# A long-convolution and MLP kernel: the second stage's table spread on chip in both halves, the second filter half turned by DMA transposes, the first inverse of half 0 on 64-row TensorE tiles

## The chip, the cores and the metric

The kernel runs on one core of one Trainium2 chip. The metric is the device time of one execution in microseconds (us). Before the change three runs gave 236.3, 236.95 and 237.21 us, a median of 236.95 us. The profile is of one execution.

## What is computed

Sequence length S = 2048, width D = 512, hidden width F = 1376, all arrays bfloat16. Two blocks A and B are applied twice, with the same weights both times:

```python
def _A_ref(q, k, v, shift_k, ssm_k, ssm_D):
    ...
    for t in range(ks):                      # ks = 4 taps
        k_shift = k_shift + k_pad[:, t:t + S, :] * shift_k[:, ks - 1 - t][None, None, :]
    kv = k_shift * v
    ...                                      # kv and ssm_k padded to 2 S, real FFTs
    y_f = kv_f * kf_f[None, :, :, :]
    y = irfft2(y_f)[..., :S, :]              # a long convolution along S, per channel
    y = y + kv * ssm_D[None, None, :]
    return q * y

def _B_ref(x, w1, b1, w2, b2):
    y = _layernorm(x, axis=-1)
    h = _gelu(einsum("bsd,df->bsf", y, w1) + b1)
    return einsum("bsf,fd->bsd", h, w2) + b2

x = A_q
x = x + _A_ref(_layernorm(x), A_k, A_v, A_shift_k, A_ssm_k, A_ssm_D)
x = x + _B_ref(_layernorm(x), B_w1, B_b1, B_w2, B_b2)
x = x + _A_ref(_layernorm(x), A_k, A_v, ...)
x = x + _B_ref(_layernorm(x), ...)
```

The convolution's result y depends on k, v and the filter only, so it is computed once and used by both A blocks.

## The kernel before

**Halves.** The sequence is split into two halves of 1024 positions. Half 0 needs the transform of filter half 0 and of data half 0; half 1 needs those and the transforms of filter half 1 and data half 1. Once y of half 0 is there, the LayerNorms and the MLP of half 0 run, in blocks of 128 or 256 rows, while the convolution of half 1 is computed beside them; then the MLP of half 1 runs in blocks of 512 rows.

**Stages, by the tags in the code.** `ht0`, `ht1`: the filter half is loaded with channels on the partitions and turned, 8 TensorE transposes to a tile (`turn`, L561), four tiles to a half, each copied out of PSUM by ScalarE or VectorE. `fir0` to `fir3`: the key of half 0 is turned (L610), shifted and mixed by its taps (L635) and multiplied by v (L641, VectorE). `h1_0`, `x1_0`, `h1_1`, `x1_1`: first transform stage (`stage1`, L578), eight tiles of 16 matmuls each. `h2_0`, `x2_0`, `h2_1`, `x2_1`: second stage (`stage2`, L590), eight tiles of 16 matmuls, whose weights are a table of 16384 columns in `R_S2`. A second stage's tiles 0 to 3 read its first 8192 columns and tiles 4 to 7 the others. Then come the products (L475, 128x1024 in half 0), the first inverse stage (`inverse1`, L695, tags `i1_0` and `i1_1`, eight tiles) and the second (`inverse2`, L717). ScalarE (L480) or VectorE (L481) copies each tile out of PSUM; such a copy is called an eviction here. The products also need the filter's spectrum with its real and imaginary parts exchanged, which eight DMAs make from SBUF to SBUF (`swap`, L460 `ar<-ar`).

**The table.** Every eighth block of 16 columns of `R_S2` belongs to the partitions p with p mod 8 = d, and is zero elsewhere. The compact form `C2` has 2048 columns. Before, the first half of the table is made on chip: the first 1024 columns of `C2` are loaded to `R_C` and eight instructions (tag `spread`, L519 on ScalarE, L520 on VectorE) multiply them by a mask, one for each d. The second half, 8192 columns, comes from HBM in eight loads of 256 KB (`tab_s`).

**`inverse1`** has two forms. In the whole form a tile is 16 matmuls of 128 rows by 128 columns; in the split form it is 32 matmuls on two halves of 64 rows, which write less:

```python
if split:
    for g in range(2):
        ins.append((512 * g + 4 * i, n, A(64 * g, 64, o, [4, 128]), A(64 * g, 64, R_U + n * 128 + 4 * g, [8, 16], [1, 4])))
else:
    ins.append((i * 128, n, A(0, 128, o, [4, 128]), A(0, 128, R_U + n * 128, [1, 128])))
```

Before, half 0 uses the whole form and half 1 the split one.

**What sets the order.** `Prog` records every operation. `SEQ` lists their numbers in the order in which each engine's queue is filled; `ENGS` says, one letter each, which engine takes an operation that several can do; `BANKS` gives each PSUM tile its bank. `sync` then derives the semaphore waits. Each engine works through its queue strictly in order. All large DMAs are issued by SyncE (SP), also in order, so a DMA that waits holds back those behind it. On GpSimd (POOL) each instruction waits for the one ahead of it.

**The MLP.** `m1` (L920) is the first matrix product, evicted with the GELU by ScalarE (L925); `m2` (L954) the second, added to x by VectorE (L958). The rows are normalised by L856 (ScalarE) or L857 (VectorE), after statistics by L831 and L832 (VectorE) and three small POOL instructions (L836, L838, L846). `q`, `y`, `z` are the tags of the first LayerNorm, of the multiplication with y, and of the second LayerNorm; the first two row blocks, `z0` and `z1`, are turned on TensorE (L908), all later ones by DMA transposes (L900).

Of the kernel before, what the change touches and what calls it, by code (L numbers as in the profile page):

```python
# [36 lines left out]
class Prog:  # L37
# [312 lines left out]
def _tables():  # L350
# [5 lines left out]
    a = np.arange(8)  # L356
# [12 lines left out]
    for j in range(8):  # L369
        m = np.arange(128) % 8 == pd[j]  # L370
        S2[m, :, j] = C2.reshape(128, 128, 16)[m]
    S2 = np.concatenate([C2, S2.reshape(128, 16384)], 1)
    ph = TWO_PI * k2[:, None] * a[None, :] / 8
    c, s = np.cos(ph), np.sin(ph)
    U = np.zeros((2, 8, 8, 2, 8, 2, 8))
# [23 lines left out]
def bass_interleave_layers__ssm_conv_h3__mixer_channel_mlp__prompt_kernel(  # L399
        nc, A_q, A_k, A_v, A_shift_k, A_ssm_k, A_ssm_D, B_x, B_w1, B_b1, B_w2, B_b2, out):  # L400
    P = Prog(nc)
# [593 lines left out]
```

## Time and profile before

| what | value |
|---|---|
| median of the timed runs | 236.95 us (236.3 to 237.21) |
| span of the profiled execution | 234.0 us; no other time is listed for that execution, so what lies around the span is taken as 236.95 - 234.0 = 2.95 us |
| TensorE (PE) busy | 222.7 us, 95% |
| VectorE (DVE) busy | 178.7 us, 76% |
| ScalarE (ACT) busy | 164.5 us, 70% |
| GpSimd (POOL) busy | 55.5 us, 24% |
| DMA | 24.93 MB in 40106 packets |
| granted TensorE clock | 1.00 throughout |

The span runs from the first to the last instruction. A busy share is an average over stages: in the first 60 us three engines take turns to be the last, and only the stage's own rows tell which. In a row of the timeline the numbers are the start, the time until the last of the merged instructions ended, the engine, the line, the operation, output and input, and the count; behind it stands the idle time ahead of it, with what ended it.

### The profile page before, as it was taken

Reading aid. Unit: us, or ns where it says so; the run is one execution under the profiler, and the core shown is the slowest. Engines: PE = TensorE matmul, PEld = TensorE weight load, DVE = VectorE, ACT = ScalarE, POOL = GpSimd, SP = SyncE. Lnnn points to the kernel's source line nnn. Section 1 sums busy time; section 2 is a strip of 40 time slices with the busy share of each in tenths; the row PEclk is TensorE's granted clock in tenths of the full one; section 3 lists DMA queues with packets and bytes.
Section 4 is the critical chain, followed back from the end, with each engine's and each line's share of the span. In section 5 each row is a group of like instructions: output and inputs, shape, how many; then the busy total and the mean of one; then the engine's idle time right before and its main releaser. Section 6 shows DMA issues by size and latency. Waiting matters only on the chain.

```text
span 234.0 us, 6498 instructions
## 1 busy us (share of the span) xinstructions
PE 222.7 (95%) x2743; PEld 147.1 (63%) x2765; DVE 178.7 (76%) x362; ACT 164.5 (70%) x262; POOL 55.5 (24%) x113
## 2 busy tenths in 40 slices
PE   7989887999999999999999999999999999999995
PEld 3878776967868596677966576644444444444454
DVE  0699998999999999999999988781777569410222
ACT  2789999989968688999879986488058216802710
POOL 2270132006403405639303331204011120200000
PEclk9999999999999999999999999999999999999999
DMA  6999489928994360033500313401300130170202
GB/s 185 381 386 305 147 229 274 324 65 150 144 211 126 70 158 3 1 48 72 155 4 3 90 24 68 134 3 22 69 0 3 28 62 0 23 115 0 90 0 92
DMA packets 40106, 24.93 MB, mean 107 GB/s; under 512 B 23591, under 2 KB 33677, under 8 KB 40077
## 3 DMA queue, kind: packets, MB, share of 16 engines
q1 hardware_dynamic: 39778, 24.36, 39.7%
q8 instruction: 22, 0.36, 0.7%
q10 hardware_dynamic: 298, 0.16, 0.4%
q14 instruction: 8, 0.06, 0.1%
HBM read 13.23 MB, written 2.10 MB: 66 GB/s over the span
## 4 chain that ended last, share of the span: by engine, by line
PE 58%; DVE 24%; ACT 10%; issue 2%; POOL 2%; DMA 2%; SPq 0%; DVEq 0%
PE ps L920 23%; PE ps L954 23%; DVE ar L475 13%; ACT ar L480 9%; PE ps L695 4%; DVE sm L831 3%; PE ps L590 2%; DMA ar<-in_A_ssm_k_dram 2%; DVE ar L672 2%; DVE ar L958 2%; DVE ar L641 2%; PE ps L717 1%; POOL sm L836 1%; PE ps L578 1%; PE ps L635 1%
## 5 line engine op out<-in xcount | busy, mean ns | idle before, releaser
L925 ACT ACTIVATE ar<-ps,sm 128x256 bf16<-128x256 f32 (+5 forms) x143 | 65.7, 523 | 33.2 <-PE ps L920 32.9
L920 PE MATMUL ps<-ar 128*128 128x256 bf16 (+5 forms) x569 | 81.9, 297 | 0.4 <-ACT ar L480 0.2
L480 ACT ACTIVATE ar<-ps 128x1024 bf16<-128x1024 f32 (+3 forms) x77 | 71.1, 998 | 11.0 <-PE ps L578 3.4
L954 PE MATMUL ps<-ar 128*128 128x512 bf16 (+1 forms) x323 | 75.9, 379 | 1.5 <-issue 0.6
L920 PEld LDWEIGHTS ps<-ar 128*128 128x128 bf16 (+1 forms) x572 | 52.9, 100 | 27.5 <-ACT ar L480 1.1
L475 DVE TENSOR_TENSOR ar<-ar 128x512 bf16<-128x512 bf16 (+2 forms) x104 | 62.7, 646 | 1.5 <-ACT ar L480 0.8
L954 PEld LDWEIGHTS ps<-ar 128*128 128x128 bf16 (+1 forms) x341 | 32.4, 98 | 35.3 <-ACT ar L925 0.4
L958 DVE TENSOR_TENSOR ar<-ar,ps 128x512 bf16<-128x512 bf16 x31 | 20.8, 680 | 32.9 <-PE ps L954 32.9
L831 DVE BATCH_NORM_STATS2 sm<-ar 128x6 f32<-128x512 bf16 x64 | 42.5, 685 | 0.5
L856 ACT ACTIVATE ar<-ar,sm 128x512 bf16<-128x512 bf16 x39 | 30.6, 813 | 12.9 <-DVE sm L843 8.8
L836 POOL TENSOR_SCALAR sm<-sm 128x2 f32<-128x2 f32 (+2 forms) x22 | 9.9, 449 | 89.0 <-DVE sm L832 88.8
L838 POOL TENSOR_TENSOR sm<-sm 128x2 f32<-128x2 f32 (+2 forms) x26 | 21.7, 834 | 25.1 <-DVE sm L836 23.1
L590 PE MATMUL ps<-ar 128*128 128x64 bf16 x512 | 18.4, 193 | 1.5 <-DVE ar L481 0.7
L578 PE MATMUL ps<-ar 128*64 128x128 bf16 x512 | 17.9, 221 | 1.8 <-ACT ar L480 1.2
L590 PEld LDWEIGHTS ps<-ar 128*128 128x128 bf16 x512 | 16.8, 98 | 3.6 <-DVE ar L481 1.3
L578 PEld LDWEIGHTS ps<-ar 128*64 128x64 bf16 x512 | 14.9, 110 | 4.8 <-ACT ar L480 1.9
L481 DVE CAST ar<-ps 128x1024 bf16<-128x1024 f32 x12 | 14.6, 1218 | 1.2 <-PE ps L578 0.9
L846 POOL TENSOR_SCALAR sm<-sm 128x1 f32<-128x1 f32 x34 | 15.1, 460 | 1.6
L695 PE MATMUL ps<-ar 64*128 64x64 bf16 (+1 forms) x384 | 12.4, 203 | 1.0 <-DVE ar L475 0.9
L695 PEld LDWEIGHTS ps<-ar 64*128 64x128 bf16 (+1 forms) x384 | 11.8, 113 | 2.2 <-DVE ar L475 1.0
L857 DVE TENSOR_SCALAR ar<-ar,sm 128x512 bf16<-128x512 bf16 x25 | 10.3, 415 | 2.7 <-POOL sm L846 2.5
L788 DVE SCALAR_TENSOR_TENSOR ar<-ar,sm,ps 128x512 bf16<-128x512 bf16 x16 | 11.1, 740 | 0.3 <-PE ps L590 0.3
(45 smaller groups left out, 93.5 us busy)
## 6 DMA issues: line engine op xcount, KB each, us to landing
ar<-ar SPq DMA_DIRECT2D x16, 256.0 KB, 4.0
ar<-tab_s SPq DMA_DIRECT2D x9, 256.0 KB, 6.3
ar<-in_A_ssm_k_dram SPq DMA_DIRECT2D x8, 256.0 KB, 5.9
ar<-in_A_q_dram SPq DMA_DIRECT2D x8, 256.0 KB, 4.4
ar<-in_A_v_dram SPq DMA_DIRECT2D x8, 256.0 KB, 5.0
out_dram<-ar SPq DMA_DIRECT2D x7, 256.0 KB, 2.5
ar<-in_B_w_dram SPq DMA_DIRECT2D x4, 344.0 KB, 5.2
ar<-in_B_w_dram SPq DMA_DIRECT2D x5, 256.0 KB, 5.2
```

The source lines that it names most:

```text
L475: return P.op(eng, lambda e: e.tensor_tensor(o, a, b, op), dur, reads=[a, b] + list(more), writes=[o])
L480: return e.activation(dst, src(), AF.Copy)
L578: r = e.matmul(Q(tl, 64 * ri, 64, i * 128, [1, 128]), w, m, start=True, stop=True)
L590: r = e.matmul(Q(tl, 0, 128, i // 8 * 512 + i % 8 * 4, [32, 16], [1, 4]), w, m, start=True, stop=True)
L695: r = e.matmul(Q(tl, 0, 128, i, *([32, 16], [1, 4]) if split else ([1, 128],)), w, m, start=n == 0, stop=n == 1)
L831: P.op(DVE, lambda e, sj=sj, x=x: e.bn_stats(sj, x), 600.0, reads=[x], writes=[sj])
L838: P.op(POOL, lambda e: e.tensor_tensor(r, v, hf, ALU.pow), 420.0 + 149.0 * n, reads=[v, hf], writes=[r])
L856: return e.activation(o, x, AF.Identity, bias=u, scale=r)
L920: r = e.matmul(Q(tl, 0, rows, 0, [1, w]), a, m, start=dk == 0, stop=dk == 3)
L925: P.op(ACT, lambda e, dst=dst, tl=tl, rows=rows, bias=bias, w=w: e.activation(dst, Q(tl, 0, rows, 0, [1, w]), AF.Gelu_apprx_tanh, bias=bia ...
L954: r = e.matmul(Q(tl, 0, 128, 0, [1, 512]), ins[fc][0], ins[fc][1], start=fc == 0, stop=fc == 10)
L958: P.op(DVE, lambda e, x=x, tl=tl: e.tensor_tensor(x, x, Q(tl, 0, 128, 0, [1, 512]), ALU.add), 604.0, reads=[x], writes=[x], tile=tl)
```

## The change

1. **Table.** Both halves of `R_S2` are spread on chip. The eight loads of the second half go; one load of the other 1024 compact columns comes. There are 16 `spread` instructions in place of 8, and POOL is now among the engines that can run them.
2. **Filter half 1.** `turn(1, ...)`, with its four TensorE tiles of 8 transposes and their four evictions, is replaced: the load puts the rows in another order, four POOL copies (tag `hcopy`, 128x1024, read with a stride of 8 elements) gather them into `R_Y0`, and eight DMA transposes, two to a copy, turn them into `R_HP1`. `h1_1` reads its weights from there with a stride.
3. **First inverse of half 0** uses the split form.
4. `SEQ`, `ENGS` and `BANKS` are new throughout. Lines move by 6 to 13 in the file (L590 is L596 after, L695 is L701, L475 is L476).

```diff
     SEQ = (
-        0, 46, 8, 45, 35, 2, 6, 3, 5, 36, 12, 9, 1, 10, 11, 25, 4, 44, 217, 7, 56, 197, 15, 50, 16, 57, 14, 13, 47,
...
+        44, 36, 46, 37, 45, 9, 0, 18, 1, 38, 47, 57, 39, 43, 40, 41, 3, 6, 2, 48, 58, 59, 7, 51, 4, 74, 22, 202, 221,
...
-    S2 = np.concatenate([C2, S2.reshape(128, 16384)], 1)
+    S2 = C2
...
     def load_h(half, o):
         for b in range(4):
-            dma(A(0, 128, o + b * 1024, [1, 1024]), dr(A_ssm_k, b * 128 * 2048 + 1024 * half, [2048, 128], [1, 1024]), 1 << 18, paced=True)
+            rows = [[2048, 128]] if not half else [[2048, 8], [8 * 2048, 16]]
+            dma(A(0, 128, o + b * 1024, [1, 1024]), dr(A_ssm_k, b * 128 * 2048 + 1024 * half, *rows, [1, 1024]), 1 << 18, paced=True)
...
-    tload(t_s2, 18432, 0, R_C, 1024)
+    wide = 2048
+    for h in range(2):
+        tload(t_s2, wide, 1024 * h, R_C + 1024 * h, 1024)
...
-    for i in range(8, 16):
-        tload(t_s2, 18432, 2048 + i * 1024, R_S2 + i * 1024, 1024)
...
-    for h in range(1):
+    for h in range(2):
         for d in range(8):
...
-            P.op(BOTH, f, {ACT: 912.0, DVE: 395.0}, reads=[c, m], writes=[o])
+            P.op((ACT, DVE, POOL), f, {ACT: 1040.0, DVE: 395.0, POOL: 1050.0}, reads=[c, m], writes=[o])
...
-    turn(1, R_HRAW1, R_HP1)
+    P.tag = "hcopy"
+    for b in range(4):
+        o, x = A(0, 128, R_Y0 + 1024 * b, [128, 8], [1, 128]), A(0, 128, R_HRAW1 + 1024 * b, [1, 8], [8, 128])
+        P.op(POOL, lambda e, o=o, x=x: e.tensor_copy(o, x), 1050.0, reads=[x], writes=[o])
+    P.tag = "ht1"
+    for b in range(4):
+        for i in range(2):
+            x, o = A(0, 128, R_Y0 + 1024 * b + 512 * i, [1, 512]), A(0, 128, R_HP1 + 1024 * b + 512 * i, [128, 4], [1, 128])
+            P.op(SP, lambda e, x=x, o=o: e.dma_start_transpose(o, x), 1300.0, reads=[x], writes=[o], dma=True, nbytes=1 << 17)
+    lhs = lambda g: A(0, 128, R_HP1 + 1024 * (g // 16) + g % 16, [16, 64])
     P.tag = "h1_1"
-    stage1(lambda g: A(0, 128, R_HP1 + 64 * g, [1, 64]), R_G1)
+    stage1(lhs, R_G1)
...
-    inverse1(R_1, R_2, R_3, False)
+    inverse1(R_1, R_2, R_3, 1)
```

The key's eight DMA transposes of half 1 move into a function `turn_k`, called once at the same place.

Three places show what the new order does. **POOL, ahead of the second stage.** Before, behind the last of the bias additions to the filter (L475, 1x16x8) and of the tap products (L548), POOL has only small work:

```order
L475 TENSOR_TENSOR ar<-ar 1x16x8
L548 TENSOR_TENSOR ar<-ar 128x256
L624 COPY ar<-ar 128x3
L836 TENSOR_SCALAR sm<-sm 128x1
L838 TENSOR_TENSOR sm<-sm 128x1
L624 COPY ar<-ar 128x3
L838 TENSOR_TENSOR sm<-sm 128x1
```

After the change the same stretch of POOL's queue holds spreads (L526, 128x64x16) and gathering copies (L753, 128x1024):

```order
L526 TENSOR_SCALAR ar<-ar,sm 128x64x16 x2
L849 TENSOR_SCALAR sm<-sm 128x1
L851 TENSOR_TENSOR sm<-sm 128x1
L859 TENSOR_SCALAR sm<-sm 128x1
L788 CAST sm<-ar 128x1
L526 TENSOR_SCALAR ar<-ar,sm 128x64x16
L630 COPY ar<-ar 128x3
L476 TENSOR_TENSOR ar<-ar 1x16x8
L526 TENSOR_SCALAR ar<-ar,sm 128x64x16 x3
L753 COPY ar<-ar 128x1024
L526 TENSOR_SCALAR ar<-ar,sm 128x64x16 x5
L849 TENSOR_SCALAR sm<-sm 128x2
```

Eleven of the 16 spreads now stand on POOL, four on DVE and one on ACT (before, six on DVE and two on ACT). The first three and the first of the run of three complete POOL's part of the table's first half; the other seven, with one gathering copy among them, complete its part of the second.

**SP, around the eight exchanges** (`ar<-ar 64x8x256`). Before, they go out in two groups of four, with loads between and behind them:

```order
L460 DMA ar<-in_A_ssm_k_dram 128x1024
L460 DMA ar<-in_B_b_dram 96x1
L460 DMA ar<-ar 64x8x256 x4
L460 DMA ar<-in_B_w_dram 128x2x512
L460 DMA ar<-ar 64x8x256 x4
L470 DMA ar<-tab_small 128x1024
```

After the change the DMA transposes of the filter (L758) stand among them:

```order
L758 DMA_TRANSPOSE ar<-ar 128x4x128
L461 DMA ar<-in_B_b_dram 96x1
L461 DMA ar<-ar 64x8x256 x4
L758 DMA_TRANSPOSE ar<-ar 128x4x128 x2
L461 DMA ar<-ar 64x8x256 x3
L758 DMA_TRANSPOSE ar<-ar 128x4x128 x2
L461 DMA ar<-ar 64x8x256
L461 DMA ar<-in_B_w_dram 128x1376
```

Two transposes are now ahead of the second group, and four ahead of the last exchange.

**PE, from the second stage to the second inverse.** Before (L590 second stage, L578 first stage of filter half 1, L561 its transposes, L695 first inverse, L717 second inverse):

```order
L590 MATMUL ps<-ar 128x16x4 x48
L578 MATMUL ps<-ar 64x128 x64
L561 MATMUL ps<-ar 128x128 x8
L695 MATMUL ps<-ar 128x128 x128
L578 MATMUL ps<-ar 64x128 x32
L717 MATMUL ps<-ar 128x512 x2
L578 MATMUL ps<-ar 64x128 x16
L717 MATMUL ps<-ar 128x512 x14
```

After (L596, L584, L701 and L723 are the same stages):

```order
L596 MATMUL ps<-ar 128x16x4 x16
L584 MATMUL ps<-ar 64x128 x48
L701 MATMUL ps<-ar 128x16x4 x64
L584 MATMUL ps<-ar 64x128 x16
L701 MATMUL ps<-ar 128x16x4 x192
L584 MATMUL ps<-ar 64x128 x32
L723 MATMUL ps<-ar 128x512 x4
L584 MATMUL ps<-ar 64x128 x16
L723 MATMUL ps<-ar 128x512 x12
```

The last of the three first-stage tiles directly ahead of the first inverse needs the third pair of filter transposes. Behind the second inverse both programs run the same tiles, except that the turning of `z1` (L908, L921 after) now stands ahead of the first `m1` tile and stood behind it. `z0` and `z1` are normalised by ACT after the change; before, `z0` was normalised by DVE.

More of the change, by code (lines that the diff above doesn't have):

```diff
@@ L44 @@
     SEQ = (
[55 rows of a table removed]
[56 rows of a table added]
     ENGS = (
[L101 to L103 removed]
+            "vpvvappvpppppppvpvpvpvpvpaaavaavavvaaavaaavaappppaaavaaavvvaaaaaaaaavaaaavaaaavaaaaaaappppaaaaaaaaaaaaaa"
+            "aaaaaaaaaaaaaaappappaavpvppaappvvppaappaappaappaapvaappaappaapvaappaappaappavppvvppvavpavavvvvavvvvavvav"
+            "pvvvappvavavvaavapvvavapvvvvv")
     BANKS = (
[L105 to L107 removed]
+            "42272442460200460002067635640040262422640464246244600602604062234024424622264600444260620624204042204043"
+            "30461456547705110517010666612614320037722232405172756007426335436147461307413422270727065155362103103451"
+            "4060364405475615411270347042152307163024542756001300612716327433526516701532367")
     def __init__(self, nc):
@@ L502, in load_t, with turn_k @@
             dma(A(0, 128, o + 512 * a, [1, 512 * w]), dr(x, 512 * (1024 * half + a), [8 * 512, 128], [1, 512 * w]), w << 17, paced=True)
-    tload(t_s2, 18432, 0, R_C, 1024)
+    wide = 2048
+    for h in range(2):
+        tload(t_s2, wide, 1024 * h, R_C + 1024 * h, 1024)
     load_h(0, R_1)
+    def turn_k(half):
+        for a in range(8):
+            src, dst = dr(A_k, 512 * (1024 * half + a), [8 * 512, 128], [1, 512]), A(0, 128, R_KT + 144 * a + 16, [1152, 4], [1, 128])
+            P.op(SP, lambda e, src=src, dst=dst: e.dma_start_transpose(dst, src), 1300.0, writes=[dst], dma=True, nbytes=1 << 17)
     load_t(A_k, 0, R_8, 2)
     load_t(A_v, 0, R_8 + 4096, 2)
-    for i in range(8, 16):
-        tload(t_s2, 18432, 2048 + i * 1024, R_S2 + i * 1024, 1024)
     P.tag = "spread"
@@ L797, in bass_interleave_layers__ssm_conv_h3__mixer_channel_mlp__prompt_kernel @@
     P.tag = "kt"
-    for a in range(8):
-        src, dst = dr(A_k, 512 * (1024 + a), [8 * 512, 128], [1, 512]), A(0, 128, R_KT + 144 * a + 16, [1152, 4], [1, 128])
-        P.op(SP, lambda e, src=src, dst=dst: e.dma_start_transpose(dst, src), 1300.0, writes=[dst], dma=True, nbytes=1 << 17)
+    turn_k(1)
     for c in (0, 2):
```

6 lines of the change are left out of this document (removed), and 109 rows, old and new, of the table SEQ.

## The prediction

> **What bounds the kernel now.** I read the busy shares by stage first, then each engine's timeline around the point where the MLP begins, then single rows for prices. The first view gives the busy time of PE, PEld, DVE, ACT and POOL in six stretches (length, then busy us and count), the clock and the DMA share.
>
> ```profile
> 8.00:20.00 12.00, 11.23 (x279) 9.98 (x274) 10.77 (x20) 11.13 (x12) 4.88 (x12) 1.00 1.08 365
> 20.00:30.00 10.00, 8.74 (x227) 7.42 (x223) 9.38 (x17) 9.41 (x11) 0.93 (x3) 1.00 0.61 206
> 30.00:41.00 11.00, 8.87 (x252) 7.96 (x248) 10.18 (x15) 10.83 (x13) 3.02 (x8) 1.00 0.95 265
> 41.00:56.00 15.00, 14.08 (x241) 11.76 (x243) 14.61 (x33) 13.79 (x17) 1.91 (x5) 1.00 0.67 176
> 56.00:124.00 68.00, 66.86 (x1054) 50.65 (x1061) 67.11 (x115) 59.20 (x116) 26.09 (x42) 1.00 0.43 93
> 124.00:234.00 110.00, 106.82 (x670) 55.49 (x679) 65.57 (x166) 57.83 (x96) 16.43 (x33) 1.00 0.19 44
> ```
>
> Before 41 us PE has gaps while DVE and ACT are over 90% busy from 8 us on: there evictions and products bound the kernel. From 56 us PE is 97 to 98% busy to the end. Only a place where PE waits can give time back, or less PE work after 56 us. The next view is PE's timeline across that border.
>
> ```profile
> 41.32 7.38 PE L695 MATMUL ps<-ar 128*128 128x128 bf16 x128 [0.90 <-DVE ar L475]
> ...
> 55.37 0.40 PE L908 MATMUL ps<-ar 128*128 128x128 bf16 x4 [0.28 <-ACT ar L480]
> ...
> 56.46 0.84 PE L920 MATMUL ps<-ar 128*128 128x128 bf16 x12 [0.22 <-ACT ar L480]
> ```
>
> The first inverse (L695) starts at 41.32 us, when a product (DVE L475) lets it; the first MLP matmul (L920) at 56.46, on an ACT eviction. Behind that matmul the two programs have the same PE work, but for `z1`'s four transposes (L908, 0.40 us for `z0`), which the change puts ahead of it. So **the end moves with the first L920**, as far as PE stays as full behind it. What decides that start is on ACT and DVE, whose timelines are next.
>
> ```profile
> 30.37 17.65 ACT L480 ACTIVATE ar<-ps 128x1024 bf16<-128x1024 f32 x19 [0.17 <-PE ps L590]
> 48.73 6.59 ACT L480 ACTIVATE ar<-ps 128x1024 bf16<-128x1024 f32 x8 [0.71 <-PE ps L695]
> 55.81 0.60 ACT L480 ACTIVATE ar<-ps 128x512 bf16<-128x512 bf16 x1 [0.49 <-PE ps L908]
> 56.30 0.80 ACT L856 ACTIVATE ar<-ar,sm 128x512 bf16<-128x512 bf16 x1
> ```
>
> ```profile
> 36.35 8.52 DVE L475 TENSOR_TENSOR ar<-ar 128x1024 bf16<-128x1024 bf16 x14 [0.82 <-ACT ar L480]
> ```
>
> ACT runs 19 evictions in 17.65 us (0.93 us each) and, after a gap, eight more to 55.32; then the turn of `z0` is evicted and the MLP starts. DVE's last 14 products run without a gap from 36.35 to 44.87.
>
> **The change, part by part.** All sums are made against the profiled execution: its span of 234.0 us, which with the 2.95 us around it stands for the median of 236.95. The rows for the removed and added work:
>
> ```profile
> L561 PE MATMUL ps<-ar 128*128 128x128 bf16 x64 | 6.2, 252 | 0.6 <-DMA ar<-in_A_ssm_k_dram 0.3 <-ACT ar L480 0.3
> L695 PE MATMUL ps<-ar 128*128 128x128 bf16 x128 | 7.4, 219 | 0.9 <-DVE ar L475 0.9
> L695 PE MATMUL ps<-ar 64*128 64x64 bf16 x256 | 5.0, 194 | 0.1
> L480 ACT ACTIVATE ar<-ps 128x1024 bf16<-128x1024 bf16 x5 | 5.2, 1037 | 2.6 <-PE ps L561 2.6
> L481 DVE COPY ar<-ps 128x1024 bf16<-128x1024 bf16 x7 | 4.8, 683 | 7.6 <-PE ps L561 6.9 <-PE ps L610 0.7
> L480 ACT ACTIVATE ar<-ps 128x512 bf16<-128x512 f32 x4 | 2.3, 606 | 0.0
> L519 ACT ACTIVATE ar<-ar,sm 128x1024 bf16<-128x1024 bf16 x2 | 2.3, 1164 | 0.0
> L520 DVE TENSOR_SCALAR ar<-ar,sm 128x1024 bf16<-128x1024 bf16 x6 | 3.0, 512 | 0.0
> ```
>
> *PE.* The filter turn of half 1 goes: half of L561's 6.2 us, less its waits, some 2.5 to 3 us. The first inverse of half 0 in the split form costs what half 1's does, 5.0 in place of 7.4: 2.4 us. Together about 5 us, all ahead of 56 us, where it counts only if PE is last.
>
> *ACT.* Up to the last eviction of the second inverse the new assignment takes off two evictions of each filter turn (4 x 1.04), one spread (1.16), one of `h1_0` and one of `h1_1` (2 x 0.93), and adds two of the key's turn (2 x 1.04) and one of `x1_0` (0.93): 4.2 us less. *DVE.* Up to its last product it loses two spreads (1.0), two evictions of filter turn 1, two of the key's turn and one of `x1_0`, and gains two of filter turn 0, one of `h1_0`, one of `h1_1` and a row of statistics: about 1.0 us less. So ACT's saving is the larger, but the products, on DVE, hold the first inverse.
>
> *The table's second half.* Seven of its eight spreads are on POOL, behind four of the first half. No POOL row shows a spread. The nearest rows:
>
> ```profile
> L872 POOL MEMSET ar<- x4: 306/412/519, 58.0 to 160.1; 1x256 bf16 x2, 1x512 bf16 x2
> L768 POOL CAST sm<-ar x2: 183/188/193, 28.1 to 30.1; 128x10 f32<-128x10 bf16 x1, 96x1 f32<-96x1 bf16 x1
> L548 POOL TENSOR_TENSOR ar<-ar x4: 612/612/612, 12.2 to 15.3; 128x256 bf16<-128x256 bf16 x4
> 8.40 0.42 POOL L475 TENSOR_TENSOR ar<-ar 1x128 bf16<-1x128 bf16 x1 [0.59 <-DVE ar L481]
> 28.51 2.76 PE L590 MATMUL ps<-ar 128*128 128x64 bf16 x80
> ```
>
> A memset takes (519 - 306)/256 = 0.83 ns per element; 1024 of them behind a cast's 0.19 us give **1.04 us**, and 0.94 with the memset's own start (306 - 256 x 0.83 = 0.09) is the lower end. The two-input L548 gives (612 - 190)/256 = 1.65 ns, so 1.88 us as upper end. A spread reads one array, as a cast does: I take 1.05, for the gathering copies too. POOL's tap products and bias additions end near 9.8 us (three L475 end at 8.82, and some of the L548 now stand ahead of them). Up to the last spread it then has 11 spreads, one gathering copy and 2.7 us of small work: 9.8 + 12 x 1.05 + 2.7 = 25.1 us. The second half of the table is first read in L590's run at 28.51, which may come 2 us sooner. So it is in time, by 1 to 3 us, and the limit is (28.5 - 9.8 - 2.7)/12 = 1.33 us a spread. The other three gathering copies end near 27, 29 and 30 us. The Trainium skill (GPSIMD Engine Reference, section "Elementwise — side-by-side cycle accounting") speaks against that: it gives about 2.6 cycles per element, which at its 1.2 GHz would be an estimate of 2.2 us, and by it the sum would be 9.8 + 12 x 2.2 + 2.7 = 39 us and the second stage some 10 us late; that is the second rival below, taken further.
>
> The other price is that POOL and DVE hold each other up:
>
> ```profile
> 90.16 3.48 DVE L475 TENSOR_TENSOR ar<-ar 128x2048 bf16<-128x2048 bf16 x3
> 90.35 3.34 POOL L836 TENSOR_SCALAR sm<-sm 128x2 f32<-128x2 f32 x1 [8.07 <-DVE sm L832]
> 12.22 1.99 POOL L548 TENSOR_TENSOR ar<-ar 128x256 bf16<-128x256 bf16 x3 [3.07 <-DVE ar L481]
> 13.82 0.68 DVE L520 TENSOR_SCALAR ar<-ar,sm 128x1024 bf16<-128x1024 bf16 x1
> 15.33 0.61 POOL L548 TENSOR_TENSOR ar<-ar 128x256 bf16<-128x256 bf16 x1
> 15.35 1.23 DVE L641 TENSOR_TENSOR ar<-ps,ar 128x1024 bf16<-128x1024 f32 x1
> 16.89 1.22 DVE L641 TENSOR_TENSOR ar<-ps,ar 128x1024 bf16<-128x1024 f32 x1
> ```
>
> A two-element POOL instruction lasted 3.34 us, exactly as long as DVE's three products beside it; and the DVE spread at 13.82, begun while POOL worked until 14.21, took 0.68 us where the six have a mean of 0.51. Now four DVE spreads stand beside POOL's long run: up to 4 x 1.05 us if each waits for a whole POOL spread, and not below nothing, since a wait saves no time; I take 0.7 in all, four times the 0.17 by which the spread at 13.82 was longer. DVE's reads from PSUM, most of its work there, show no such stretch: L641 took 1.23 us beside POOL's L548 and 1.22 without. The Trainium skill (SBUF — State Buffer, section "Who interferes with whom") calls it an exclusive lock on a shared port pair, held for the whole instruction; the 3.34 us agree, and by it DVE would pay towards the upper end.
>
> *The DMAs.* Seven loads fewer (8 go, 1 comes), in a stretch with a DMA share of 1.08; the loads of v keep their places in SP's queue, so their arrival does not move. Eight transposes come:
>
> ```profile
> 28.48 3.28 SPq L460 DMA_DIRECT2D ar<-ar  x4
> ar<-ar SPq DMA_DIRECT2D x8, 256.0 KB, 4.5
> ar<-ar SPq DMA_TRANSPOSE x30, 2.5
> L900 SPq DMA_TRANSPOSE ar<-ar x30: 1188/1264/2244, 64.3 to 206.7; - x30
> ```
>
> An exchange occupies SP for 0.8 us and lands 4.5 us after its issue; a transpose 1.26 and 2.5. With the evictions that release the first group 1.5 us sooner: exchanges 27.0 to 30.3, transposes to 32.8, three exchanges to 35.2, the third pair to 37.7, the last exchange to 38.5. That one lands at 37.7 + 4.5 = 42.2. DVE's last product would end at 44.87 - 1.0 + 0.7 = 44.6 and the last four (0.61 each) begin at 42.2, so it is just in time; the third pair at 39 to 41. The last `h1_1` tile ahead of the first inverse waits for that pair, so I take 40.9 us for the first inverse (before 41.32): the DVE saving is mostly used up by it.
>
> *From there to the MLP.* First eviction at 40.9 + 0.6 = 41.5. Up to the end of the second inverse ACT has six evictions of the first inverse, three of `h1_1` and five of the second (two short ones, 2.3/4 = 0.57): 12 x 0.93 + 1.15 = 12.3 us, to 53.8 against 55.32: **-1.5**. Then `z0`: before, from 55.32 to 56.46, an eviction; now ACT also normalises (0.80), PE turns (0.40), ACT evicts (0.60), 0.2 of hand-over: 2.0 us, **+0.9**. The first L920 comes at 55.8, -0.6; with `z1`'s transposes ahead, **-0.3** more of PE. Sum -0.9 us: 236.95 - 0.9 = 236.05, so **236.0 us**. The 5 us of PE work mostly become idle time on PE, for ACT's chain is last there.
>
> **Rivals.** *The saving passes through.* If the products run on DVE's time alone and no transpose is late, the first L920 moves with ACT's sum, 4.2 - 0.9, and with -0.3: 236.95 - 3.6 = 233.4. For it: DVE and PE have less to do as well; against it: the third pair of transposes and POOL's queue. *POOL is late* (the other side): POOL paces the second table half from 1.33 us a spread on. At 1.6 us, by rate or by DVE's holding it, the second stage comes 12 x 0.27 = 3.2 us late: 236.05 + 3.2 = 239.3; at 1.88 us 242.7. For it: L548's rate and the 3.34 us; against it: cast and memset. *SP is late*: if a transpose occupies SP for 1.75 us, halfway between L900's median and its longest, the four ahead of the last exchange add 4 x 0.49 = 2.0 us, the last four products wait for that exchange, and the second half of the first inverse for them: 236.05 + 2.0 = 238.0. For it: SP's queue of DMAs; against it: the median. The change might also not shorten the split inverse in half 0; hidden behind ACT, that would cost nothing.
>
> **How the numbers follow.** A measurement of this kernel can tell about 0.5% from no change: 235.8 to 238.1. Forecast 0.48 (234.8 to 237.3 by its terms; 0.20 of it faster, 0.28 the same), saving through 0.20 (faster), POOL late 0.20 (slower), SP late 0.12 (half the same, half slower). That gives faster 0.40, same 0.34, slower 0.26. The range is 233.2 to 241.5: it leaves out the upper end of POOL's price and the far end of the saving, about 1 in 10 on either side.
>
> **What would show it.** Right: POOL's spreads near 1.05 us; no PE wait on POOL at the second stage; the first L920 near 55.8; ACT without gaps from 41 to 56; PE over 97% busy behind it. Wrong: POOL spreads of 1.4 us or more, DVE spreads near 1.5, the tile behind the third pair of transposes waiting past 42 us, or PE gaps behind 56 us, where new idle time would cost in full.

## The result: 10.8% slower, and the profile after

| | median | runs | span of the profiled execution |
|---|---|---|---|
| before | 236.62 us (235.6 to 237.21) | 4 | 234.0 us |
| after | 261.45 us (260.85 to 263.18) | 4 | 261.4 us |

The ratio is 1.1078, with a 95% interval of 1.1028 to 1.1128 (of the fast runs, since some executions fall in a second, slower state; it is not the quotient of the two medians). The forecast was 236.0 us and its range ended at 241.5. The profiled execution after is the run of 263.18 us, so 1.8 us lie around its span, and about as much in every run here whose span is listed. The 2.95 us that the prediction took for the execution before are therefore some 1.1 us too many: the span of 234.0 belongs to a run of about 235.8 us. No term of its sum hangs on that.

The first view of the changed kernel is the busy time by stage, with the columns of the prediction's first view (length, then busy us and count of PE, PEld, DVE, ACT and POOL, the clock, the DMA share, GB/s).

```profile
20.00:32.00 12.00, 10.87 (x262) 9.35 (x264) 7.97 (x11) 8.65 (x10) 11.27 (x8) 0.86 0.13 43
32.00:46.00 14.00, 0.37 (x14) 0.20 (x8) 2.28 (x3) 1.51 (x2) 13.63 (x5) 0.60 0.75 156
...
81.00:150.00 69.00, 67.18 (x1034) 50.03 (x1031) 66.16 (x115) 59.06 (x118) 18.72 (x38) 1.00 0.38 85
```

From 32 to 46 us PE, DVE and ACT do next to nothing and only POOL works: this stretch did not exist before. POOL's timeline shows what it does there.

```profile
9.71 5.84 POOL L526 TENSOR_SCALAR ar<-ar,sm 128x1024 bf16<-128x1024 bf16 x2
...
21.06 8.71 POOL L526 TENSOR_SCALAR ar<-ar,sm 128x1024 bf16<-128x1024 bf16 x3
29.84 2.05 POOL L753 COPY ar<-ar 128x1024 bf16<-128x1024 bf16 x1
31.98 14.58 POOL L526 TENSOR_SCALAR ar<-ar,sm 128x1024 bf16<-128x1024 bf16 x5
```

The groups of L526 (minimum, median and maximum in ns, first and last start):

```profile
L526 POOL TENSOR_SCALAR ar<-ar,sm x11: 2842/2842/2892, 9.7 to 43.7; 128x1024 bf16<-128x1024 bf16 x11
L526 DVE TENSOR_SCALAR ar<-ar,sm x4: 472/605/1341, 12.4 to 27.6; 128x1024 bf16<-128x1024 bf16 x4
```

A spread takes 2.85 us on POOL, and the last one ends at 46.56. PE's timeline has the answer to it:

```profile
21.01 1.92 PE L584 MATMUL ps<-ar 128*64 128x128 bf16 x32 [4.71 <-POOL ar L476]
...
46.62 5.29 PE L596 MATMUL ps<-ar 128*128 128x64 bf16 x96 [14.25 <-POOL ar L526]
...
61.28 1.25 PE L701 MATMUL ps<-ar 64*128 64x64 bf16 x64 [0.33 <-DVE ar L476]
...
69.76 0.90 PE L701 MATMUL ps<-ar 64*128 64x64 bf16 x27 [2.43 <-issue]
...
81.56 3.10 PE L933 MATMUL ps<-ar 128*96 128x128 bf16 x52
```

The second stage waits 14.25 us for POOL; a bias addition that stands behind a spread in POOL's queue had already held PE for 4.71 us. So the first inverse starts at 61.28 (41.32 before) and the MLP at 81.56 (56.46). From there to the end it takes 261.4 - 81.56 = 179.8 us against 234.0 - 56.46 = 177.5: of the 27.4 us between the two spans 25.1 are lost ahead of the first MLP matmul and 2.3 behind it.

### The profile page after: what moved, and what is told of

Same layout as the page of the kernel before. It is cut to its first block, busy times and chain, and to the rows that moved or that the text cites. A ratio compares the mean times of both kernels' runs of the same rounds, so it can differ in the third digit from the quotient of the medians.

```text
span 261.4 us, 6728 instructions
## 1 busy us (share of the span) xinstructions
PE 229.4 (88%) x2861; PEld 150.1 (57%) x2861; DVE 181.0 (69%) x356; ACT 161.6 (62%) x258; POOL 91.2 (35%) x134
## 4 chain that ended last, share of the span: by engine, by line
PE 51%; DVE 19%; POOL 19%; ACT 5%; issue 4%; DMA 1%; SPq 0%; POOLq 0%; DVEq 0%
PE ps L933 21%; PE ps L967 20%; POOL ar L526 12%; DVE ar L476 11%; DVE sm L844 4%; ACT ar L481 3%; PE ps L596 2%; POOL sm L859 2%; PE ps L584 2%; PE ps L701 2%; DMA ar<-ar 1%; POOL sm L851 1%; PE ps L538 1%; DVE ar L971 1%; DVE ar L678 1%
## 5 line engine op out<-in xcount | busy, mean ns | idle before, releaser
L938 ACT ACTIVATE ar<-ps,sm 128x256 bf16<-128x256 f32 (+4 forms) x143 | 65.2, 524 | 44.3 <-PE ps L933 44.1
L967 PE MATMUL ps<-ar 128*128 128x512 bf16 (+1 forms) x341 | 78.0, 379 | 0.0
L476 DVE TENSOR_TENSOR ar<-ar 128x512 bf16<-128x512 bf16 (+2 forms) x104 | 64.3, 659 | 3.4 <-ACT ar L481 2.9
L849 POOL TENSOR_SCALAR sm<-sm 128x2 f32<-128x2 f32 (+2 forms) x20 | 4.9, 243 | 91.2 <-DVE sm L845 90.7
L596 PE MATMUL ps<-ar 128*128 128x64 bf16 x512 | 20.3, 202 | 16.5 <-POOL ar L526 14.2
L526 POOL TENSOR_SCALAR ar<-ar,sm 128x1024 bf16<-128x1024 bf16 x11 | 31.3, 2849 | 1.1
L596 PEld LDWEIGHTS ps<-ar 128*128 128x128 bf16 x512 | 18.9, 104 | 18.4 <-POOL ar L526 14.4
L584 PE MATMUL ps<-ar 128*64 128x128 bf16 x512 | 23.1, 247 | 5.8 <-POOL ar L476 4.9
L584 PEld LDWEIGHTS ps<-ar 128*64 128x64 bf16 x512 | 20.1, 140 | 9.3 <-POOL ar L476 5.4
L701 PE MATMUL ps<-ar 64*128 64x64 bf16 x512 | 10.3, 197 | 3.2 <-issue 2.6
L701 PEld LDWEIGHTS ps<-ar 64*128 64x128 bf16 x512 | 9.4, 114 | 5.1 <-issue 3.2
```

The lines of the kernel that those rows point to most:

```text
L476: return P.op(eng, lambda e: e.tensor_tensor(o, a, b, op), dur, reads=[a, b] + list(more), writes=[o])
L526: return e.tensor_scalar(o, c, m, None, ALU.mult)
L584: r = e.matmul(Q(tl, 64 * ri, 64, i * 128, [1, 128]), w, m, start=True, stop=True)
L596: r = e.matmul(Q(tl, 0, 128, i // 8 * 512 + i % 8 * 4, [32, 16], [1, 4]), w, m, start=True, stop=True)
L701: r = e.matmul(Q(tl, 0, 128, i, *([32, 16], [1, 4]) if split else ([1, 128],)), w, m, start=n == 0, stop=n == 1)
L938: P.op(ACT, lambda e, dst=dst, tl=tl, rows=rows, bias=bias, w=w: e.activation(dst, Q(tl, 0, rows, 0, [1, w]), AF.Gelu_apprx_tanh, bias=bia ...
```

## The experiments

A range after a median is that of its runs; a ratio is against the kernel before, run beside it, with its 95% interval.

**1. All spreads off POOL.** The 11 spreads that POOL had go to DVE, nothing else moves.

```diff
-            "vpvvappvpppppppvpvpvpvpvpaaavaa...
+            "vvvvavvvvvvvvvvvvvpvpvpvpaaavaa...
```

> The changed kernel with its eleven POOL spreads given to DVE (0.48 us each by L520 of the kernel before), in the same order; nothing else differs. Theory A, POOL's price alone: a spread took 2.85 us there instead of the 1.05 of my sum, PE waited 14.2 us for the last one, and the clock fell behind that wait. Then the wait goes, DVE gets 11 x 0.48 = 5.3 us more in front of the products, and the time is 236 to 241 us, with the clock at 1.00 throughout. Theory B, the filter transposes on SP and the new order cost several us of their own: 243 us or more, with PE waits on DMA or on a transpose ahead of the first inverse.

Measured: 246.87 us (245.26 to 248.72), 1.0419 (1.0377 to 1.0461). 14.6 us come back, but 10.3 stay; the first MLP matmul is at 67.12. POOL's price is the largest part and not the whole.

**2. The split inverse alone, in the kernel before.**

```diff
-    inverse1(R_1, R_2, R_3, False)
+    inverse1(R_1, R_2, R_3, True)
```

> The kernel before with only the first inverse of half 0 in the split form; order, engines and banks as before. My sum took the 2.4 us of PE work as hidden behind ACT, since ACT has evictions without a gap from 41 to 55 us: 236.6 us, no change. Rival: PE is last in that stage (L695 runs 7.38 us without a gap from 41.32), and the first MLP matmul comes up to 2.3 us sooner: 234.3 us.

Measured: 237.8 us (235.32 to 239.01) against 236.55, 1.0031 (1.0003 to 1.0059): no gain, and 0.3% or 0.7 us more if anything. The PE time saved becomes idle time, as forecast: between its groups the split inverse waits 0.15 to 0.58 us for evictions and products, and the first MLP matmul of the profile is at 57.51 (56.46 before).

**3. What POOL takes for such instructions**, each three or four times, alone and beside DVE.

```diff
+    P.op(POOL, lambda e: e.tensor_scalar(st(0), c3, m, None, ALU.mult), ...)
+    P.op(POOL, lambda e: e.tensor_copy(st(0), c3), ...)
+    P.op(POOL, lambda e: e.tensor_copy(gw, g8), ...)
```

> Not the computation: a list of single POOL operations, three times each, with DVE idle, then four spreads beside DVE products and four gathering copies beside DVE spreads. Its output is constants, and its time means nothing. Theory rate: a one-input POOL operation with arithmetic takes 2.7 to 2.8 ns per element whatever its strides, so the spread is 2.85 us with DVE idle too, contiguous or not, and 0.7 to 0.8 us at 256 elements; the copy 2.0 us; only the memset runs at 0.83. Theory stride: a contiguous spread takes 1.05 us and the strided one 2.85. Theory contention: 1.05 us alone and longer beside DVE.

The groups of this kernel, POOL only (busy us, mean ns of one):

```profile
L463 POOL TENSOR_SCALAR ar<-ar,sm 128x1024 bf16<-128x1024 bf16 x4 | 15.0, 3748 | 0.8 <-DVE ar L461 0.6
L446 POOL TENSOR_SCALAR ar<-ar,sm 128x1024 bf16<-128x1024 bf16 x3 | 8.5, 2846 | 11.4 <-DVE ar L435 11.2
L447 POOL TENSOR_SCALAR ar<-ar,sm 128x1024 bf16<-128x1024 bf16 x3 | 8.5, 2844 | 0.3
...
L454 POOL COPY ar<-ar 128x1024 bf16<-128x1024 bf16 x3 | 5.9, 1973 | 0.2
L456 POOL TENSOR_TENSOR ar<-ar 128x1024 bf16<-128x1024 bf16 x3 | 5.7, 1892 | 0.2
...
L453 POOL COPY ar<-ar 128x1024 bf16<-128x1024 bf16 x3 | 3.1, 1041 | 0.2
L452 POOL COPY ar<-ar 128x1024 bf16<-128x1024 bf16 x3 | 3.1, 1037 | 0.2
L457 POOL MEMSET ar<- 128x1024 bf16 x3 | 2.9, 952 | 0.2
```

L446 is the spread with its strided output, L447 the same contiguous: 2.85 us both, so the stride costs nothing. A memset takes 0.95 and a copy 1.04, as the prediction worked out; but the multiplication by a scalar takes 2.85, more than one by a second array (L456, 1.89). The gathering copy (L454) takes 1.97. L463 is the spread beside DVE's products: 3.75.

**4. The wait filled with PE work.** PE's granted clock has a mean of 0.60 in the stretch of the POOL wait (32 to 46 us, above). 64 matmuls of zeros are put ahead of the waiting tile.

```diff
+        tl = stage2(R_2, t, 64 if t == 7 else 0)
...
+                for i in range(fill):
+                    r = e.matmul(Q(tl, 0, 128, 0, [1, 512]), z[:, :128], z, start=True, stop=True)
```

> The changed kernel with 64 matmuls of 128x512 on zeros put on PE in front of the second-stage tile that waited 14.2 us for POOL, so that PE is busy through most of that wait (13.7 us); their results are overwritten. Theory clock: the granted clock stays at 1.00 from 32 to 56 us and the work behind the wait runs at full speed; 3 to 5 us less than the changed kernel's 261.45, so 256 to 258.5. Rival: the low clock falls together with waits on evictions and costs nothing: 261 to 262 us.

Measured: 260.96 us (259.87 to 262.03), 1.1037 (1.1 to 1.1074). The clock stays at 1.00 from 32 to 56 us, and the median falls by 0.5 us, which is less than the runs differ among each other. So the low clock in that wait is not what the kernel loses by. It is not shown that a low clock costs nothing: in this run it fell to 0.50 later, from 60 to 64 us, while PE was working.

```profile
32.00:48.00 16.00, 15.43 (x116) 7.72 (x119) 2.52 (x5) 2.19 (x3) 15.26 (x10) 1.00 0.61 136
```

```profile
60.00:64.00 4.00, 3.59 (x88) 3.32 (x90) 4.00 (x7) 1.27 (x2) 0.00 (x0) 0.50 1.11 330
```

**5. Experiment 1 with the filter turned on TensorE again.**

```diff
-    P.tag = "hcopy"
...
-            P.op(SP, lambda e, x=x, o=o: e.dma_start_transpose(o, x), ...)
-    stage1(lhs, R_G1)
+    turn(1, R_HRAW1, R_HP1)
+    stage1(lambda g: A(0, 128, R_HP1 + 64 * g, [1, 64]), R_G1)
```

> The kernel of the first experiment (all spreads off POOL, 246.87 us, 10.3 over the kernel before) with one thing undone: the second filter half is loaded as before and turned on TensorE with four evictions (two on ACT, two on DVE), so that the four gathering copies on POOL and the eight DMA transposes are gone; the new order else. Theory T (what is left of the loss is the turn's chain: POOL copies of about 2.05 us, transposes of 3 us each in front of the exchanges, two waits of 1.42 and 1.20 us on PE): at least half of the 10.3 us goes, 237 to 241.5 us, and the first matmul of the MLP comes 5 us earlier than 67.1. Theory D (the 11 spreads that DVE took over, 5 us of its time in a stretch that is full): the time stays within 2 us of 246.9, since DVE gets two evictions more. Theory S (the stall of 2.4 us inside the split inverse and the low clock behind it): within 2 us of 246.9 too, the stall stays.

Measured: 242.91 us (241.62 to 243.82), 1.0282 (1.0236 to 1.0328). Of the 10.3 us, 4 go; theory T wanted 5 or more, and both others wanted none. The MLP starts at 61.97, 5.15 us earlier, as T had it, and the stall inside the split inverse shrank from 2.44 to 0.23 us.

**6. Experiment 1 with the whole inverse.**

```diff
-    inverse1(R_1, R_2, R_3, 1)
+    inverse1(R_1, R_2, R_3, 0)
```

> The kernel of the first experiment (246.87 us) with one thing undone: the first inverse of half 0 in its whole form (128 matmuls of 128 rows in place of 256 of 64). Theory S (the stall of 2.4 us in which PE waited for nothing that the trace shows, in the middle of the split matmuls, belongs to that form): the stall is gone or moves, and the time falls by 2 to 4 us, to 243 to 245. Theories T and D: within 1 us of 246.9, and the stall, if it hangs on the count of instructions on PE and not on their form, stands at about the 985th matmul again, wherever that is now (128 matmuls later in the program).

Measured: 246.29 us (245.63 to 247.44), 1.0434 (1.0393 to 1.0476): no gain that can be told. The stall was gone in the one profile (0.16 us the longest), and the MLP started there at 64.25 against 67.12, but the medians do not follow: experiment 1's profile is its slowest run (248.72 us).

**7. The 11 spreads shared, 7 to DVE and 4 to ACT.**

```diff
-            "vpvvappvpppppppvpvpvpvpvp...
+            "vvvvavvavavvvavvavpvpvpvp...
```

> The changed kernel with its 11 POOL spreads shared, 7 to DVE and 4 to ACT (the first experiment gave all 11 to DVE: 246.87). Theory D (DVE's extra 5 us in a full stretch is what is left of the loss): 242 to 245, since ACT's spread costs about 0.9 us against DVE's 0.5 but ACT has gaps there. Theories T and S: 246 to 249, no gain.

Measured: 246.39 us (245.16 to 247.38), 1.0447 (1.0399 to 1.0496), 1.4 us above theory D's range. That does not clear DVE: a spread took 1.15 us on ACT and not the 0.9 expected (the rows of before had 1.16), and the second stage now waits 2.23 us for the last one there. Experiment 10 tests the spreads on DVE by themselves.

**8. The transposes alone, in the kernel before.** The load, the copies and the transposes are those of the change, in the old order.

```diff
-    turn(1, R_HRAW1, R_HP1)
+    P.tag = "hcopy"
...
+            P.op(SP, lambda e, x=x, o=o: e.dma_start_transpose(o, x), ...)
+    lhs = lambda g: A(0, 128, R_HP1 + 1024 * (g // 16) + g % 16, [16, 64])
```

> The kernel before (236.6) with only the second filter half changed: rows of that half loaded 8 apart, four gathering copies on POOL, eight DMA transposes on SP, in place of 32 transposes on PE and four evictions; everything else and its order as before (copies and transposes some 25 places earlier than the turn stood, one transpose of k behind its reader). Theory T: the chain costs by itself, 239 to 243 us, with PE waits on the transposes in the trace. Theories D and S: 235 to 237.5, since POOL is free here and ACT and DVE lose four evictions (about 2.6 us).

Measured: 243.59 us (243.32 to 244.69), 1.0324 (1.0286 to 1.0361). That is just above theory T's range. The part that was to spare PE and ACT their work **costs 7.4 us by itself**, with the rest of POOL's and DVE's work as before. SP's timeline of this kernel:

```profile
24.82 3.84 SPq L751 DMA_TRANSPOSE ar<-ar  x2
...
29.34 2.54 SPq L751 DMA_TRANSPOSE ar<-ar  x2
31.93 3.21 SPq L460 DMA_DIRECT2D ar<-ar  x4
35.18 2.88 SPq L751 DMA_TRANSPOSE ar<-ar  x2
...
38.80 3.17 SPq L460 DMA_DIRECT2D ar<-ar  x4
```

and that of the kernel before:

```profile
28.48 3.28 SPq L460 DMA_DIRECT2D ar<-ar  x4
...
33.25 3.21 SPq L460 DMA_DIRECT2D ar<-ar  x4
```

The exchanges (`ar<-ar`, four at a time) are issued 3.45 and 5.55 us later, behind transposes. DVE's products wait for them (behind one, an eviction that PE then waits 4.05 us for) and end 5.4 us later, at 50.24 against 44.87. The first MLP matmul is 7.8 us later (64.23 against 56.46); the other 2.4 were not taken apart. The first row of those products, and the row of all eight transposes on SP (minimum, median and maximum in ns):

```profile
37.32 2.93 DVE L475 TENSOR_TENSOR ar<-ar 128x1024 bf16<-128x1024 bf16 x2 [3.16 <-DMA ar<-ar]
```

```profile
L751 SPq DMA_TRANSPOSE ar<-ar x8: 1234/1273/2533, 24.8 to 44.5; - x8
```

**9. The forecast's price put in place.** POOL's 11 spreads become plain copies.

```diff
+                if e is nc.gpsimd:
+                    return e.tensor_copy(o, c)
                 return e.tensor_scalar(o, c, m, None, ALU.mult)
```

> The changed kernel with its 11 POOL spreads replaced by plain POOL copies of the same tile into the same places (1.04 us in the pricing run, where the spread took 2.85); the mask is left out on POOL, so the second stage's table is not the one of the reference. All else, the order too, is as in the changed kernel. This puts the forecast's price (1.05 us) in place of the real one. If the price was the only step that failed: 233 to 241.5 us, the range of the prediction. If the turn's chain (4.0 us between the first and the fifth experiment) and whatever else is left of the loss (about 6 us) stand beside it, less the 5 us of spreads that DVE is spared against the first experiment: 241 to 245 us, no PE wait on a spread, and PE waits of 1 us or more on the transposes.

Measured: 248.2 us (248.11 to 249.57), 1.0518 (1.0478 to 1.0558). The copies took 1.04 us (L527 below), 13.2 us came back, PE waits 0.2 us on them, and yet the kernel is 12 us over the one before: more than either expectation had. Its copies, two rows of PE, and SP's queue:

```profile
L527 POOL COPY ar<-ar x11: 1035/1036/1113, 10.1 to 28.6; 128x1024 bf16<-128x1024 bf16 x11
```

```profile
40.30 1.23 PE L586 MATMUL ps<-ar 128*64 128x128 bf16 x16 [4.23 <-DMA ar<-ar]
...
55.09 0.70 PE L703 MATMUL ps<-ar 64*128 64x64 bf16 x27 [2.98 <-issue]
```

```profile
30.02 3.70 SPq L461 DMA_DIRECT2D ar<-ar  x4
33.77 3.03 SPq L760 DMA_TRANSPOSE ar<-ar  x2
36.90 2.58 SPq L461 DMA_DIRECT2D ar<-ar  x3
39.53 2.74 SPq L760 DMA_TRANSPOSE ar<-ar  x2
42.31 0.60 SPq L461 DMA_DIRECT2D ar<-ar  x1
```

PE's 4.23 us are a wait for a transfer that L586, the first stage, reads: transposed data. With the transposes' median of 4.7 us from issue to landing (20 to 46 us, the row below) the pair issued from 33.77 on is the one that lands near 40.

```profile
ar<-ar SPq DMA_TRANSPOSE x7, 4.7
```

**10. The table's second half spread on chip alone**, in the order of before, by eight more DVE spreads.

```diff
-    for h in range(1):
+    for h in range(2):
...
-            "pvavvvvv...
+            "pvavvvvvavvvvvvvv...
```

> The kernel before (236.2) with only the first part: the second half of the table spread on chip from a second compact load (eight loads of 256 KB are gone), by eight more spreads on DVE (0.48 us each, 3.8 us), placed between its products ahead of the second half's first use; order, turn and inverse as before. If what is left in the fifth experiment (6.7 us over the kernel before) is the spreads on the engine that bounds this stretch: 239 to 242 us, first matmul of the MLP 3 us or more later than 56.5. If it is the new order: 235 to 237.5.

Measured: 239.73 us (238.73 to 239.99), 1.0138 (1.0095 to 1.0182): 3.5 us for 8 x 0.48 = 3.8 us of DVE time. The first MLP matmul is at 60.20, 3.7 us later, and PE's second stage waits for the last of the spreads:

```profile
31.89 4.52 PE L589 MATMUL ps<-ar 128*128 128x64 bf16 x96 [2.24 <-DVE ar L519]
```

In the stage where DVE is over 90% busy, and at these places in its queue, the spreads cost nearly their whole duration.

**11. The new order alone.** Experiment 5 with the second half loaded again.

```diff
-    S2 = C2
+    S2 = np.concatenate([C2, S2.reshape(128, 16384)], 1)
...
+    for i in range(8, 16):
+        tload(t_s2, 18432, 2048 + i * 1024, R_S2 + i * 1024, 1024)
```

> The kernel of the fifth experiment (242.9; turn on TensorE, all spreads off POOL, new order, split inverse) with the table's second half loaded again in eight loads, as in the kernel before, so that the eight spreads of that half are gone from DVE. What is left of the change is the new order and the split inverse, which cost 0.3 us in the second experiment. If the spreads make the loss: 236 to 239 us. If the new order (with its choice of engines) makes it: 240.5 to 243.5.

Measured: 241.17 us (239.4 to 242.84), 1.0206 (1.0142 to 1.0269). The new order with its engines and the split inverse (0.3% or 0.7 us in experiment 2, not 0.3 us) costs 5.0 us without any of the new work; since it has no places for the turn's four tiles on TensorE, those stand where experiment 5 put them, and what that placing costs is in the 5.0. So each of experiments 10 and 11 came out as the theory that blames its part has it: the spreads on DVE and the order both cost.

**12. Experiment 8 without the gathering copies.** Four short POOL copies (16 columns each) stand in their places.

```diff
-            x, o = A(0, 128, R_Y0 + 1024 * b + 512 * i, [1, 512]), A(
+            x, o = A(0, 128, R_HRAW1 + 1024 * b + 512 * i, [1, 512]), A(
```

> The kernel of the eighth experiment (the kernel before with the DMA transposes alone, 243.59 us, 7.4 over before) without the gathering copies on POOL: the transposes read the loaded rows directly, so that channels come out in another order than the reference's (the filter's second half is wrong by a permutation; the shapes and the work on the other engines are the same). Theory C (the loss is the chain: a copy of 2.05 us, behind what POOL does first, in front of each pair): the transposes are issued from 22 us on, where SP was idle until 28.5 in the kernel before, the exchanges keep their place, and most of the loss goes: 236 to 239.5 us. Theory Q (the loss is the transposes themselves: 3 us of SP for a pair in front of exchanges, and some 500 short packets each on the DMA engines): 241 to 244.5, and the exchanges still land late.

Measured: 243.8 us (242.95 to 244.34), 1.0315 (1.0285 to 1.0345), the same as with the copies. Theory C falls. SP's timeline again:

```profile
25.92 3.74 SPq L751 DMA_TRANSPOSE ar<-ar  x2
...
30.33 2.79 SPq L751 DMA_TRANSPOSE ar<-ar  x2
33.17 3.21 SPq L460 DMA_DIRECT2D ar<-ar  x4
36.42 2.87 SPq L751 DMA_TRANSPOSE ar<-ar  x2
...
40.03 3.17 SPq L460 DMA_DIRECT2D ar<-ar  x4
```

Here SP issues six transposes in 3.74 + 2.79 + 2.87 = 9.4 us ahead of the last exchanges. It begins them at 25.92, behind the loads that its queue still holds, although nothing on POOL delays them. The exchanges land in 4.4 us, as before (4.5): they are late because they are issued late. (The filter half is loaded with its rows 8 apart in both experiments; what that alone does was not run.)

**13. Both put right: copies for spreads, and the turn on TensorE.**

```diff
+                if e is nc.gpsimd:
+                    return e.tensor_copy(o, c)
...
+    turn(1, R_HRAW1, R_HP1)
```

> The kernel of the ninth experiment (POOL's spreads as plain copies of 1.04 us, mask left out, 248.2 us) with the second filter half turned on TensorE again as in the fifth. If the turn's chain is what made the ninth miss, the time falls by 6 us or more, to 239 to 242, near the new order alone (241.2). If POOL's copies cost by slowing DVE beside them, or by their place in POOL's queue, it stays at 243 or more.

Measured: 240.84 us (240.09 to 240.99), 1.0195 (1.0171 to 1.0219), within 0.4 us of the new order alone. With the spread's price and the transposes put right, the time is that of the new order without the second half's spreads (11): 11 of them at 1.04 us on POOL cost nothing that can be told. SP then issues the eight exchanges from 25.91 us on, without a break:

```profile
25.91 9.03 SPq L460 DMA_DIRECT2D ar<-ar  x8
```

and rows of PE up to the MLP, with ACT's last evictions ahead of it:

```profile
41.91 0.72 PE L702 MATMUL ps<-ar 64*128 64x64 bf16 x32
43.17 0.72 PE L568 MATMUL ps<-ar 128*128 128x128 bf16 x8 [0.54 <-ACT ar L480]
...
56.81 0.40 PE L914 MATMUL ps<-ar 128*128 128x128 bf16 x4 [1.11 <-ACT ar L862]
...
58.13 3.10 PE L926 MATMUL ps<-ar 128*96 128x128 bf16 x52
```

```profile
44.58 11.49 ACT L480 ACTIVATE ar<-ps 128x1024 bf16<-128x1024 f32 x13 [0.55 <-PE ps L702]
55.89 1.70 ACT L862 ACTIVATE ar<-ar,sm 128x512 bf16<-128x512 bf16 x2
```

## Why the prediction was wrong, step by step

The loss splits along experiments 9 and 13, each with one thing less:

| step | time | what it took away |
|---|---|---|
| the changed kernel | 261.45 us | |
| POOL's spread at 1.04 us (9) | 248.2 us | 13.2 us: the price of the spread |
| and the turn on TensorE (13) | 240.84 us | 7.4 us: the DMA transposes |
| the kernel before | 236.2 us | 4.6 us: the order, with the split inverse and the turn's tiles put into it |

The transposes and the order were each measured a second time in another setting: the transposes alone 7.4 us (8), the order alone 5.0 (11). The parts do not simply add up. With the spreads on DVE, undoing the transposes gave back only 4.0 us (experiment 1 to 5). And of the 7.4 us between 9 and 13 up to 2.8 may be the stall described at the end (2.98 against 0.20 us in the profiles).

- *What bounds the kernel* ("the end moves with the first L920") **held, but for 2.3 of 27.4 us**. Between the two profiles the first MLP matmul moved by 25.1 us and the end by 27.4. Behind that matmul the new order added 2.3 to 2.6 us (238.2 - 58.13 = 180.1 in experiment 13 against 177.5), where PE waits 2.2 us for ACT (0.2 before); the prediction had put PE gaps there among what would make it wrong.
- *The table's second half*: **this step failed, and by its price alone.** "A spread reads one array, as a cast does: I take 1.05." The runs show 2.85, outside both ends (0.94 and 1.88). The sum itself was right: with 11 spreads at 2.85 and a gather at 2.05 it gives 9.8 + 31.4 + 2.05 + 2.7 = 45.9 us, and POOL ended at 46.56. The rival "POOL is late" named mechanism and threshold (1.33 us a spread), and stopped at 242.7 because its price stopped at 1.88. No neighbour shared the instruction's kind: of memset, cast and two-input product none is an arithmetic with a scalar. The POOL rows that are (L836) have 1 to 4 elements and a median of 0.19 us, from which no rate can be read. The rate from the Trainium skill (GPSIMD Engine Reference, section "Elementwise — side-by-side cycle accounting"), an estimate of 2.2 us in the prediction, was the nearest of all, but by luck: that section traces its 2.6 cycles to a two-input instruction, and the two-input one here took 1.89 us, below the estimate, the one-input spread 2.85, above it.
- *The gathering copies*, priced at 1.05 as well, took 2.04 us in the changed kernel. In the kernel before, with POOL free, taking them out saved nothing (12).
- *The DMAs*: **this step failed as well**, hidden behind the first. "That one lands at 37.7 + 4.5 = 42.2 ... so it is just in time." The issue price of a transpose was right (1.26 assumed, 1.27 the median in experiment 8), but the last of the exchanges was forecast to be issued at 37.7 and was issued at 42.31 in experiment 9; a transpose landed after 4.7 us, not 2.5. The working had SP begin the exchanges at 27.0, when their data is ready. In fact transposes and loads were still being issued: in experiment 9 the first exchange goes out at 30.02, in experiment 13, without transposes, at 25.91. The rival "SP is late" was the mechanism; its price, 2.0 us by longer issues, should have been that of the whole queue.
- *PE's 5 us*: the 2.4 of the split inverse were forecast to be hidden, and brought nothing (2). The other 2.5 to 3, of the filter turn, were not tested apart from the transposes that replaced it.
- *From there to the MLP, and ACT's 4.2 us less*: **not borne out, and tested only in part.** Experiment 13 gives two of the filter turn's evictions back to ACT (2 x 1.04 of the 4.2 us). There the first inverse starts at 41.91 (40.9 forecast, 41.32 before), ACT's last eviction ahead of `z0` ends at 44.58 + 11.49 = 56.07 (53.8 forecast, 55.32 before), and the first MLP matmul comes at 58.13 (55.8 forecast, 56.46 before). The term for `z0` was right: 2.06 us from that eviction to the MLP, where 2.0 was forecast and 1.14 stood before; it includes PE's wait of 1.11 us for ACT's normalisation. The -1.5 ahead of it did not come (+0.75, with those two evictions more on ACT). PE's 0.54 us at a tile of the filter turn (L568), which the experiment itself placed between the inverse's tiles, may be a part of that; the rest was not taken apart. So of the 4.2 us between the spans of experiment 13 and of before, 0.75 come from ACT's evictions, 0.9 from `z0` and 2.5 from behind the first MLP matmul. What ACT's saving would bring with transposes that are in time was not run.
- *DVE and POOL hold each other up*, 0.7 us taken: DVE's four spreads take 0.47 to 1.34 us in the changed kernel, 3.0 in all, so 1.1 over four at 0.48. In experiment 3 POOL's spread went from 2.85 to 3.75 us beside DVE's products, so the hold-up also runs the other way, towards POOL. The exclusive lock of the Trainium skill (SBUF — State Buffer, section "Who interferes with whom") agrees with one of these pairings only. In experiment 3 a DVE spread beside a gathering copy of POOL (92.05 to 94.23) took 2.20 us and ended just behind it, at 94.52. But in the changed kernel two DVE spreads (12.76 to 14.10 and 14.03 to 14.50) lie wholly inside one POOL spread (12.66 to 15.55), which a lock held for the whole instruction would not allow. The 3.34 us of the prediction lasted through three products of DVE, 3.48 us, and not through one. What the hold-up costs the changed kernel was not measured by itself.

## What to carry to other kernels

An operation that an engine has not run yet at that size in this kernel has no price: a row of another kind of operation is no neighbour, however alike the data, and one run of a small kernel (experiment 3) gives it. A DMA is paid twice, at its landing and in the queue of the engine that issues it; list that queue in order, with every issue's duration, down to the transfer that the next stage waits for. An engine's idle time is no room for work as long as a stage waits for its results.

## What the runs showed beside that

**A stall at a fixed place of PE's stream.** PE stands still, waiting for nothing that the trace of the engines shows, when 983 to 985 matmuls and transposes have begun, counted in the timelines, in seven of these kernels: 2.43 us in the changed one, 2.44 in experiment 1, 1.36 in 7, 2.98 in 9, but 0.23 in 5 and 0.20 in 13. Experiment 4 put 64 matmuls ahead of it, and the stall moved back in the program, from ahead of the 230th matmul of the split inverse to ahead of the 167th:

```profile
67.66 1.69 PE L708 MATMUL ps<-ar 64*128 64x64 bf16 x90 [0.65 <-issue]
```

So it hangs on the count and not on the work. (In experiment 6, where it was expected too, PE waits for ACT near that count, and no stall shows.) The DMA packets tell what PE waits for. The queue that the page calls "instruction" carries 22 packets of 16 KB in the changed kernel; the last three begin when 2489, 2615 and 2741 matmuls have begun, 126 apart. And in all seven kernels PE goes on 1.3 to 1.6 us after the end of such a packet: 67.24 to 68.21 in the changed kernel, where PE goes on at 69.76; 52.55 to 53.63 in experiment 1 (55.08); 49.50 to 50.63 in 5 (52.02). So the stall reads as a wait for PE's own instructions, which come late. Why they come late was only argued: it fits that the DMA engines are full where the stall is long. In experiment 1, 52 to 54 us have a DMA share of 1.08; the two us ahead of experiment 5's stall have 0.00.

```profile
52.00:54.00 2.00, 0.63 (x38) 0.55 (x33) 1.80 (x3) 1.00 (x2) 0.58 (x3) 1.00 1.08 370
```

```profile
50.00:52.00 2.00, 1.67 (x82) 1.39 (x74) 1.85 (x4) 2.00 (x3) 1.72 (x5) 1.00 0.00 0
```

Part of what the transposes cost in the new order may come this way; in the order of before they cost the same without a stall of that size.
